# Hash attention followed by a mixture of adapters: two heads per unit in an order written by hand, 1024-column score tiles, attention output kept in SBUF, adapters run in batches inside the attention loop

## The chip, the cores and the metric

The kernel runs on one core of one Trainium2 chip. A core has a matrix engine (TensorE, PE in the profile, with its weight loads as PEld), a vector engine (VectorE, DVE), a scalar engine (ScalarE, ACT), a general engine (GpSimd, POOL), a synchronisation engine that here only starts DMA transfers (SyncE, SP), and 16 DMA engines. Each engine takes its instructions in order and waits on semaphores for what the others make. PE writes to PSUM, which has 8 banks of 2 KB per partition; the other engines empty PSUM into SBUF. The metric is device time in microseconds, and lower is better.

## What is computed

Four batches of eight heads, 768 positions, 64 features a head. Queries and keys are hashed by the signs of six projections; a query attends to the keys of its own bucket only. The 32 heads' outputs, laid side by side, are the input of a layer of eight low-rank adapters, of which each row takes the two with the highest gate.

```python
q_bits = (np.einsum('bhsd,dk->bhsk', q, proj) > 0)      # and k_bits
mask = q_bucket[:, :, :, None] == k_bucket[:, :, None, :]
scores = np.where(mask, scale * (q @ k.T), -1e9)
attn = exp(scores - max) / sum
x = (attn @ v) -> [B*S, H*D]                            # 3072 x 512
logits = x @ w_gate                                     # 8 experts, the 2 best
w = softmax of the two best logits
out = x + sum over the two: w * ((x @ A[e]) @ B[e])     # rank 16
```

## The kernel before

Everything is laid out by head, with a tile framework that decides the order of the instructions on each engine from the loops, the priorities and the pools' buffers. For each of the 32 heads the attention loop does the following. GpSimd starts three loads (vS, kS, qS; lines 81 to 85). PE transposes q and k, six blocks of 128 positions each, in float32 (lines 93 and 97); ACT copies the transposed k out of PSUM and DVE the transposed q. PE multiplies both with the projection in float32 (lines 104 and 107, 512 and 256 columns each, six output partitions), ACT takes the sign, and DVE scales it: the six scaled signs are rows 64 to 69 of kTaug and qTaug, under the 64 features in bfloat16 (lines 111 and 112). One product of 70 rows thus gives the score and a bonus that is largest where all six bits agree, and the bias neg_offset takes that bonus off again in the exponential.

The scores are made transposed, keys on the partitions: six tiles sc_ps of 128 keys by 768 queries (lines 117 and 118, 512 and 256 columns), each turned by one ACTIVATE on ACT into pTbuf (line 119). The pool of sc_ps has two buffers, so the next tile's product waits for the exponential two tiles back. Line 125 then multiplies, for each of six query blocks, six 128x128 pieces of pTbuf as weights with vS (80 columns, of which column 64 is a one and gives the row sum). DVE adds, inverts and scales (lines 130 to 134), and SP writes each 128x64 result to a DRAM tensor, x_bridge (line 135, 192 transfers).

Only behind the whole attention comes the adapter stage, in 24 tiles of 128 rows: SP reads 128x512 back (line 158), PE transposes it in four pieces (line 162) which ACT copies, then gate logits (line 167) and all eight low-rank products at once (line 174), a chain of small DVE operations for the two best gates with one exponential on ACT in it (lines 170 to 207), eight DVE scalings (line 211), a transpose (line 218), a copy on ACT, the product with B (line 222), the addition of x on DVE (line 224) and the store (line 226).

## Time and profile before

| | us |
|---|---|
| median of 3 runs | 540.51 |
| lowest and highest run | 538.18, 543.15 |
| the profiled execution's span, first to last instruction | 543.4 |
| until the first exponential starts | 18.5 |
| from there to the last sixth of the heads' loop (18.5 to 350) | 331.5 |
| the last head, alone (350 to 365) | 15.0 |
| the adapter stage (365 to the end) | 178.4 |

No time is shown for the profiled execution apart from its span; the span is 0.5% above the median of the runs. The page cuts the span into 40 slices and gives each engine's busy share of a slice in tenths, and PEclk, the TensorE clock that was granted, in tenths of its full 2.4 GHz. About the first 27 slices are attention: there PE is at 8 or 9 tenths, ACT at 5 to 8, DVE at 4 to 6, and PEclk at 6 to 9. The other 13 are the adapter stage, where PE is at 3 or 4, ACT at 1 or 2, DVE at 5 or 6, and PEclk at 5 throughout.

### The profile page before, as it was taken

The page shows a single profiled execution, that of the slowest core. Times are in us where ns is not written, and L with a number is a line of the kernel's source. Part 1 is how long each engine was busy: PE and PEld are TensorE (multiplying, and loading weights), DVE is VectorE, ACT ScalarE, POOL GpSimd, SP SyncE. Part 2 cuts the span into 40 slices and gives each one's busy share as a digit, 9 for nine tenths or more (in the row PEclk, how much of TensorE's full clock was granted, in tenths as well). Part 3 has the DMA queues.
Part 4 walks back from the last instruction along what each step waited for, and adds up shares of the span by engine and source line. Part 5 has one row for each costly group of instructions (what it writes and reads, how often), then busy time and mean ns, then how long its engine had stood idle before and what let it go on. Part 6 is the DMA issues. An engine that isn't in the chain of part 4 may idle for free.

```text
span 543.4 us, 8206 instructions
## 1 busy us (share of the span) xinstructions
PE 397.0 (73%) x2512; PEld 192.6 (35%) x2512; DVE 280.3 (52%) x1569; ACT 281.9 (52%) x529; POOL 86.3 (16%) x111
## 2 busy tenths in 40 slices
PE   4998889899999898899998998884333444433342
PEld 1444444443445444344444444342111222211121
DVE  2245546544445456345544564435656555565654
ACT  2656687857566877766657878652211222211121
POOL 9122222212112313211212221000000000000000
PEclk9999899969778999968869999855555555555555
DMA  8433343543232433423234333201222221122211
GB/s 100 50 66 60 70 69 68 114 76 67 51 60 56 76 71 77 71 54 57 54 56 76 70 71 39 27 18 54 70 79 77 77 78 66 56 74 77 77 59 40
DMA packets 68653, 35.43 MB, mean 65 GB/s; under 512 B 59264, under 2 KB 59392, under 8 KB 68608
## 3 DMA queue, kind: packets, MB, share of 16 engines
q0 software_dynamic: 34048, 16.01, 18.3%
q1 hardware_dynamic: 34560, 18.89, 12.3%
q8 instruction: 20, 0.33, 0.3%
q14 instruction: 25, 0.20, 0.1%
HBM read 25.71 MB, written 12.58 MB: 70 GB/s over the span
## 4 chain that ended last, share of the span: by engine, by line
PE 48%; ACT 28%; DVE 17%; issue 4%; DMA 1%; POOL 0%; ACTq 0%; DVEq 0%; POOLq 0%
ACT pTbuf L119 22%; PE pr L104 10%; PE ov_ps L125 9%; PE pr L107 8%; DVE zm L211 5%; PE sc_ps L117 4%; PE xT_ps L162 3%; PE d_ps L222 3%; ACT xT_sb L163 2%; PE zmT_ps L218 2%; PE z_ps L174 2%; PE tps L97 2%; PE tps L93 2%; ACT kTaug L105 2%; DVE qTaug L110 2%
## 5 line engine op out<-in xcount | busy, mean ns | idle before, releaser
L119 ACT ACTIVATE pTbuf<-sc_ps,neg_offset 128x768 bf16<-128x768 f32 x192 | 156.8, 906 | 55.1 <-PE sc_ps L118 54.7
L125 PEld LDWEIGHTS <-pTbuf 128*128 128x128 bf16 x1152 | 71.7, 107 | 130.8 <-DVE ores L134 47.9
L125 PE MATMUL ov_ps<-vS,pTbuf 128*128 128x80 bf16 x1152 | 99.6, 217 | 10.1 <-ACT pTbuf L119 7.5
L130 DVE TENSOR_SCALAR rsum<-ov_ps 128x1 f32<-128x1 f32 x192 | 26.7, 153 | 145.3 <-PE ov_ps L125 143.4
L117 PE MATMUL sc_ps<-qTaug,kTaug 70*128 70x512 bf16 x192 | 79.5, 415 | 20.5 <-ACT pTbuf L119 13.4
L218 PE MATMUL zmT_ps<-ident,zm 128*128 128x128 f32 x24 | 11.4, 474 | 89.7 <-DVE zm L211 89.7
L107 PE MATMUL pr<-qTf,proj_bf 64*6 64x256 f32 (+1 forms) x128 | 63.4, 581 | 0.0
L104 PE MATMUL pr<-kTf,proj_bf 64*6 64x256 f32 (+1 forms) x128 | 61.5, 566 | 0.0
L118 PE MATMUL sc_ps<-qTaug,kTaug 70*128 70x256 bf16 x192 | 56.3, 293 | 0.0
L134 DVE TENSOR_SCALAR ores<-ov_ps,rinv 128x64 f32<-128x64 f32 x192 | 50.6, 277 | 3.6 <-DMA x_bridge<-ores 2.6
L85 POOL DMA_DIRECT2D qS<-in_q_dram x32 | 26.6, 831 | 136.6 <-DVE rsum L130 86.4
L93 PE MATMUL tps<-ident,kS 128*64 128x128 f32 x192 | 42.0, 306 | 7.5 <-DMA kS<-in_k_dram 6.7
L105 ACT ACTIVATE kTaug<-pr 6x512 bf16<-6x512 f32 x64 | 30.6, 479 | 29.9 <-PE pr L104 28.7
L98 DVE COPY qTf<-tps 64x512 f32<-64x512 f32 x64 | 34.5, 538 | 16.2 <-PE tps L97 16.2
L219 ACT CAST zmT<-zmT_ps 128x128 bf16<-128x128 f32 x24 | 6.4, 266 | 70.2 <-PE zmT_ps L218 70.2
L108 ACT ACTIVATE qTaug<-pr 6x512 bf16<-6x512 f32 x64 | 30.6, 479 | 21.6 <-PE pr L107 20.2
L162 PE MATMUL xT_ps<-ident,xin 128*128 128x128 f32 x96 | 36.8, 435 | 3.4
L218 PEld LDWEIGHTS zmT_ps<-ident,zm 128*128 128x128 f32 x24 | 4.4, 183 | 96.0 <-DVE zm L211 96.0
L83 POOL DMA_DIRECT2D kS<-in_k_dram x32 | 26.5, 829 | 73.3 <-PE tps L93 68.6
L97 PE MATMUL tps<-ident,qS 128*64 128x128 f32 x192 | 37.7, 311 | 0.0
L163 ACT CAST xT_sb<-xT_ps 128x128 bf16<-128x128 f32 x96 | 24.3, 266 | 25.0 <-PE xT_ps L162 25.0
L224 DVE TENSOR_TENSOR acc<-d_ps,xin 128x512 f32<-128x512 f32 x24 | 16.6, 691 | 37.9 <-PE d_ps L222 37.9
(53 smaller groups left out, 443.2 us busy)
## 6 DMA issues: line engine op xcount, KB each, us to landing
kS<-in_k_dram POOLq DMA_DIRECT2D x32, 192.0 KB, 3.0
qS<-in_q_dram POOLq DMA_DIRECT2D x32, 192.0 KB, 3.1
x_bridge<-ores SPq DMA_DIRECT2D x192, 32.0 KB, 1.5
xin<-x_bridge SPq DMA_DIRECT2D x24, 256.0 KB, 2.7
out_dram<-acc SPq DMA_DIRECT2D x24, 256.0 KB, 2.0
vS<-in_v_dram POOLq DMA_DIRECT2D x32, 96.0 KB, 3.0
Acat<-in_moe_A_dram POOLq DMA_DIRECT2D x4, 32.0 KB, 3.0
Bcat<-in_moe_B_dram POOLq DMA_DIRECT2D x1, 128.0 KB, 3.2
```

The costliest lines, as they stand in the source:

```text
L93: nc.tensor.transpose(out=tps[:D, jj * P:(jj + 1) * P], in_=kS[:, j + jj, :], identity=ident)
L97: nc.tensor.transpose(out=tps[:D, jj * P:(jj + 1) * P], in_=qS[:, j + jj, :], identity=ident)
L104: nc.tensor.matmul(out=pr[:nbits, : hi - lo], lhsT=proj_bf, rhs=kTf[:, lo:hi], start=True, stop=True)
L105: nc.scalar.activation(out=kTaug[D:Daug, lo:hi], in_=pr[:nbits, : hi - lo], func=ACT.Sign, scale=1.0, bias=0.0)
L107: nc.tensor.matmul(out=pr[:nbits, : hi - lo], lhsT=proj_bf, rhs=qTf[:, lo:hi], start=True, stop=True)
L117: nc.tensor.matmul(out=sc_ps[:, :512], lhsT=kTaug[:, jk * P:(jk + 1) * P], rhs=qTaug[:, :512], start=True, stop=True)
L118: nc.tensor.matmul(out=sc_ps[:, 512:], lhsT=kTaug[:, jk * P:(jk + 1) * P], rhs=qTaug[:, 512:], start=True, stop=True)
L119: nc.scalar.activation(out=pTbuf[:, jk, :], in_=sc_ps, func=ACT.Exp, bias=neg_offset, scale=1.0)
L125: nc.tensor.matmul(out=ov_ps, lhsT=pTbuf[:, jk, iq * P:(iq + 1) * P], rhs=vS[:, jk, :], start=(jk == 0), stop=(jk == n_k_tiles - 1),)
L134: nc.vector.tensor_scalar_mul(out=ores, in0=ov_ps[:, :D], scalar1=rinv)
L162: nc.tensor.transpose(out=xT_ps, in_=xin[:, t * P:(t + 1) * P], identity=ident)
L163: nc.scalar.copy(out=xT_sb[:, t, :], in_=xT_ps)
```

## The change

The kernel is written anew as a class, Emitter, whose instructions keep the order in which they are written (the framework's scheduling is off; it still inserts the waits).

The unit is a pair of heads, 16 pairs p of 4 per batch. A pair's scores are 12 key tiles of 768 queries, taken as one row of 9216 columns and cut into nine slots of 1024 columns (two PSUM banks): score(p, s) makes two or three products and one ACTIVATE of 128x1024. PSUM: two buffers of two banks for the scores (tag s), two of one bank for transposes and hashes (tag t), one bank for the attention output (tag v) and one for all of the adapters (tag m). ACT does nothing but exponentials.

Between the slots' scores stands the other work, by slot s of pair p: s 0 and 1, transposes of pair p+1; s 2, 4, 5, the attention product of the second head of pair p-1 (14 products each); s 3, the hash of p+1; s 6, the first transposes of p+2 and a transpose of the finished output of p-2; s 7 and 8, the attention product of the first head of p (21 each). The casts, copies and normalisations on DVE go with them.

Parts of the computation change form. Two blocks of 64 features are transposed at once (128x128, 12 per pair instead of 24). The hash is four float32 products of 384 columns, each with 32 output partitions at its own strip of PSUM; DVE makes plus and minus one half of it in one operation, and eight small DMA transfers on SP's queue put the six sign rows under the features in `aug`. The feature scaling sits in the cast and in the exponential's scale, and a constant row replaces the bias. A seventh product per query block, with the constant eps as weights and the sum of v, is added. The output is normalised for six blocks at once into x, in SBUF; x_bridge is gone. v and x are cast on GpSimd. SP issues the loads, GpSimd only those of the adapter weights.

The adapters run on a batch of 768 rows, for batch b at pairs 4b+6 and 4b+7 (batches 0 to 2), and for batch 3 behind the loop: gate and low-rank products in one of 136 columns (lgz, three row blocks at a time), the gating for three blocks at once (route: DVE's max, two comparisons, an exponential on ACT, a product, three scalings), six transposes (zmtrans), and six times a product of 512 columns with one DVE operation (delta), each on the one bank of tag m.

```diff
+    def hash(self, p):
+        ps = self.ps_t.tile([self.P, 384], F32, tag="t", name=f"hs{p}")
+        for j in range(4):
+            nc.tensor.matmul(out=ps[32 * j:32 * j + 32, :], lhsT=self.proj2,
+                             rhs=self.qkT[p][:, j * 384:(j + 1) * 384], start=True, stop=True)
...
+        nc.vector.tensor_scalar(out=sgn, in0=ps, scalar1=0.0, scalar2=0.5,
+                                op0=ALU.is_gt, op1=ALU.subtract)
...
+        for j in range(4):
+            av = aug[64:70, j, :].rearrange("p (u e c) -> p u e c", e=2, c=self.P)
+            for e in range(2):
+                nc.sync.dma_start(out=av[:, :, e, :],
+                                  in_=sgn[32 * j + 6 * e:32 * j + 6 * e + 6, :].rearrange(
+                                      "p (u c) -> p u c", c=self.P))
...
+    def score(self, p, s):
...
+        ps = self.ps_s.tile([P, 1024], F32, tag="s", name=f"s{p}_{s}")
...
+            n = min(512 - at % 512, S - q0)
...
+        nc.scalar.activation(out=self.P_[p][:, s * 1024:end], in_=ps, func=ACT.Exp, scale=128.0)
...
+    def delta(self, b, i):
...
+        ps = self.ps_m.tile([P, self.Dm], F32, tag="m", name=f"dl{b}_{i}")
+        nc.tensor.matmul(out=ps, lhsT=self.zmT[b][:, i * P:(i + 1) * P], rhs=self.Bcat,
+                         start=True, stop=True)
+        nc.vector.scalar_tensor_tensor(out=self.acc[b][:, i, :], in0=ps, scalar=self.rt[b][:, i:i + 1],
+                                       in1=self.x[b][:, i, :], op0=ALU.mult, op1=ALU.add)
...
+    def moe_slot(self, p, s):
+        o = p - 2
+        if o >= 0 and o % self.PPB == 0 and o // self.PPB >= 1:
+            b = o // self.PPB - 1
+            if s in (1, 3):
+                self.lgz(b, s // 2)
+            if s in (2, 4):
+                self.route(b, s // 2 - 1)
+            if s == 5:
+                self.zmtrans(b)
+        o = p - 3
+        if o >= 0 and o % self.PPB == 0 and o // self.PPB >= 1:
+            b = o // self.PPB - 1
+            if s < 6:
+                self.delta(b, s)
...
+        for p in range(N):
+            for s in range(9):
+                self.score(p, s)
+                if s == 0:
+                    self.load(p + 2)
+                    self.norm(p - 1, 0)
+                    self.trans(p + 1, 1)
+                if s == 1:
+                    self.trans(p + 1, 2)
+                    self.vcast(p + 1)
+                if s == 2:
+                    self.pvmm(p - 1, 1, 0, 2)
+                    self.cast(p + 1, 0)
+                if s == 3:
+                    self.hash(p + 1)
+                if s == 4:
+                    self.pvmm(p - 1, 1, 2, 4)
+                    self.cast(p + 1, 1)
+                if s == 5:
+                    self.pvmm(p - 1, 1, 4, 6)
+                    self.norm(p - 1, 1)
+                if s == 6:
+                    self.trans(p + 2, 0)
+                    self.xtrans(p - 2)
+                if s == 7:
+                    self.pvmm(p, 0, 0, 3)
+                if s == 8:
+                    self.pvmm(p, 0, 3, 6)
+                self.moe_slot(p, s)
+        p = N - 1
+        self.norm(p, 0)
+        self.pvmm(p, 1, 0, 6)
+        self.norm(p, 1)
+        self.xtrans(p - 1)
+        self.xtrans(p)
+        b = self.B - 1
+        for g in range(2):
+            self.lgz(b, g)
+            self.route(b, g)
+        self.zmtrans(b)
+        for i in range(6):
+            self.delta(b, i)
```

On PE, before, the projection products of a head to come stand among the products of line 125, where the scheduler put them:

```order
L125 LDWEIGHTS pTbuf
L125 MATMUL ov_ps<-vS,pTbuf 128x80
L104 MATMUL pr<-kTf,proj_bf 6x256
L107 MATMUL pr<-qTf,proj_bf 6x256
L125 LDWEIGHTS pTbuf
L125 MATMUL ov_ps<-vS,pTbuf 128x80
```

After, in slots 3 and 4 of pair 1 (s is a score tile, hs the hash of pair 2, pv the output of pair 0):

```order
L190 LDWEIGHTS aug_106
L190 MATMUL s_3_382<-aug_106 128x512
L190 LDWEIGHTS aug_106
L190 MATMUL s_3_382<-aug_106 128x256
L190 LDWEIGHTS aug_106
L190 MATMUL s_3_382<-aug_106 128x256
L155 MATMUL hs_387<-qkT_263,proj_95 32x384 x4
L190 LDWEIGHTS aug_106
L190 MATMUL s_4_402<-aug_106 128x512
```

The four hash products now stand together, and the next slot's scores stand right behind them.

On DVE, before, one adapter tile's gating is a run of its own, nothing of the attention in it (20 instructions with the eight of line 211):

```order
L187 TENSOR_TENSOR l_6925<-l_6925,logits 128x8
L189 TENSOR_REDUCE m_6928<-l_6925 128x1
L191 TENSOR_SCALAR is_6930<-l_6925,m_6928 128x8
L197 TENSOR_SCALAR ssum<-w2p 128x1
L199 RECIPROCAL rinv<-ssum 128x1
```

After, in slots 2 to 4 of pair 6 (aug is the cast of pair 7, sgn its signs, lz and zm the adapters of batch 0):

```order
L172 TENSOR_SCALAR aug_106<-qkT_1208 64x12x128
L264 MAX top_0_1347<-lz_0_1311 128x8 x3
L266 TENSOR_TENSOR d_0_1351<-lz_0_1311,top_0_1347 128x24
L269 TENSOR_TENSOR m_0_1353<-lz_0_1311,top_0_1347 128x24
L274 TENSOR_TENSOR gw_0_1357<-m_0_1353,e_0_1355 128x24
L276 TENSOR_TENSOR zm_1345<-lz_0_1311,gw_0_1357 128x128 x3
L281 TENSOR_REDUCE ss_0_1362<-gw_0_1357 128x3
L282 RECIPROCAL rt_1346<-ss_0_1362 128x3
L158 TENSOR_SCALAR sgn_1375<-hs_1370 128x384
L172 TENSOR_SCALAR aug_106<-qkT_1208 64x12x128
```

A gating for 384 rows is now ten instructions between the two casts of the next pair, ahead of that pair's signs.

On SP, after, in slots 0 and 3 of each pair (the first three are the loads of pair p+2, the last the sign rows of pair p+1):

```order
L114 DMA nat_195<-in_q_dram 128x2x384
L114 DMA nat_195<-in_k_dram 128x2x384
L117 DMA vn_198<-in_v_dram 128x2x384
L164 DMA aug_106<-sgn_238 6x3x128 x8
L114 DMA nat_328<-in_q_dram 128x2x384
```

SP had one kind of transfer in the attention loop before, x_bridge; it now has these eleven per pair.

## Rows read from the trace of the kernel before

**Rows 1.** The page's first part: span, busy time, share of span and instructions.

```profile
span 543.4 us, 8206 instructions
PE 397.0 (73%) x2512; PEld 192.6 (35%) x2512; DVE 280.3 (52%) x1569; ACT 281.9 (52%) x529; POOL 86.3 (16%) x111
```

**Rows 2.** Windows by stage: length, busy PE, PEld, DVE, ACT, POOL (x instructions), PEclk, DMA.

```profile
18.50:350.00 331.50, 303.38 (x2067) 146.46 (x2065) 166.00 (x934) 233.57 (x367) 73.00 (x88) 0.90 0.35 65
365.00:543.40 178.40, 68.95 (x337) 35.46 (x336) 104.49 (x585) 35.56 (x140) 0.00 (x0) 0.50 0.20 67
```

**Rows 3.** Timeline of the adapter stage: start, length, instruction, [idle before].

```profile
480.48 0.61 PE L222 MATMUL d_ps<-Bcat,zmT 128*128 128x512 bf16 x1 [0.20 <-ACT zmT L219]
...
481.12 0.69 DVE L224 TENSOR_TENSOR acc<-d_ps,xin 128x512 f32<-128x512 f32 x1 [1.58 <-PE d_ps L222]
...
481.84 0.34 SPq L226 DMA_DIRECT2D out_dram<-acc  x1
...
486.92 0.48 PE L218 MATMUL zmT_ps<-ident,zm 128*128 128x128 f32 x1 [3.80 <-DVE zm L211]
```

**Rows 4.** Timeline, one head's run of exponentials: ACT, and PE within it.

```profile
205.31 4.86 ACT L119 ACTIVATE pTbuf<-sc_ps,neg_offset 128x768 bf16<-128x768 f32 x6 [1.44 <-PE sc_ps L118]
...
207.05 0.38 PE L117 MATMUL sc_ps<-qTaug,kTaug 70*128 70x512 bf16 x1 [0.23 <-ACT pTbuf L119]
...
207.27 0.27 PE L118 MATMUL sc_ps<-qTaug,kTaug 70*128 70x256 bf16 x1
...
207.38 0.24 PE L125 MATMUL ov_ps<-vS,pTbuf 128*128 128x80 bf16 x2
```

**Rows 5.** Groups of instructions by form, ACT: xcount, busy us, mean ns, idle before.

```profile
L119 ACT ACTIVATE pTbuf<-sc_ps,neg_offset 128x768 bf16<-128x768 f32 x192 | 156.8, 906 | 55.1 <-PE sc_ps L118 54.7
...
L108 ACT ACTIVATE qTaug<-pr 6x512 bf16<-6x512 f32 x32 | 18.7, 585 | 14.0 <-PE pr L107 14.0
...
L108 ACT ACTIVATE qTaug<-pr 6x256 bf16<-6x256 f32 x32 | 11.9, 372 | 7.6 <-PE pr L107 6.2
```

**Rows 6.** Timeline, PE between two runs of exponentials.

```profile
201.91 0.60 PE L125 MATMUL ov_ps<-vS,pTbuf 128*128 128x80 bf16 x12
...
202.44 0.59 PE L104 MATMUL pr<-kTf,proj_bf 64*6 64x256 f32 x2
...
202.87 0.59 PE L107 MATMUL pr<-qTf,proj_bf 64*6 64x256 f32 x2
...
205.55 0.60 PE L97 MATMUL tps<-ident,qS 128*64 128x128 f32 x4
```

**Rows 7.** Groups by form, DVE and one of POOL, columns as in rows 5.

```profile
L98 DVE COPY qTf<-tps 64x512 f32<-64x512 f32 x32 | 21.7, 679 | 13.6 <-PE tps L97 13.6
...
L112 DVE TENSOR_SCALAR qTaug<-qTf 64x768 bf16<-64x768 f32 x32 | 17.5, 547 | 0.0
...
L182 DVE TENSOR_REDUCE m<-logits 128x1 f32<-128x8 f32 x24 | 3.9, 161 | 0.8
...
masks.py:197 POOL MEMSET ident<- 128x128 f32 x1 | 0.2, 204 | 0.3 <-POOLq L241 0.3
```

**Rows 8.** DMA issues by line: xcount, KB each, median us from issue to landing.

```profile
kS<-in_k_dram POOLq DMA_DIRECT2D x32, 192.0 KB, 3.0
...
x_bridge<-ores SPq DMA_DIRECT2D x192, 32.0 KB, 1.5
```

**Rows 9.** Windows of 1 us around a fall of the granted clock, columns as in rows 2.

```profile
108.00:109.00 1.00, 0.98 (x8) 0.56 (x8) 0.00 (x0) 1.00 (x2) 0.00 (x0) 1.00 1.47 227
...
110.00:111.00 1.00, 1.00 (x2) 0.00 (x0) 0.00 (x0) 0.69 (x2) 0.00 (x0) 0.50 0.85 182
```

**Rows 10.** Timeline, the kernel's beginning.

```profile
6.70 1.03 PE L93 MATMUL tps<-ident,kS 128*64 128x128 f32 x4 [6.70 <-DMA kS<-in_k_dram]
...
11.53 0.94 DVE L112 TENSOR_SCALAR qTaug<-qTf 64x768 bf16<-64x768 f32 x1
...
13.85 1.06 PE L104 MATMUL pr<-kTf,proj_bf 64*6 64x256 f32 x2
```

425 lines of the change are left out of this document (252 added, 173 removed).

## Prediction

> **What bounds the kernel now.** I read the page's first part, then the windows by stage, then the timeline inside one stretch of each stage. The page alone misleads: PE is busy for 73% of 543.4 us and DVE and ACT for 52% each [rows 1], but these are means over two stages. The windows separate them [rows 2]. The attention loop (331.5 us from the first exponential, 18.5, to 350, then a last head of 15) has PE at 92%, ACT at 70%. The adapter stage takes 178.4 us, a third of the span, with no engine over 60% and the clock at 0.50, the lower level of 1.2 GHz.
>
> The adapter stage is a latency chain: 24 tiles of 128 rows in 178.4 us are 7.4 each, and in each PE waits 3.80 for DVE's small operations before it can transpose their result in L218 [rows 2, 3].
>
> The attention loop alternates. In a run of six exponentials (4.86 us) ACT sets the pace, and PE is held back: the products L117 wait for an exponential [rows 4]. Between the runs ACT waits for the projections and signs of the next head. A head is (331.5+15)/32 = 10.8 us on average, of which exponentials are 4.9; its 192 ACTIVATEs are 156.8 busy of ACT's 281.9 [rows 1, 5]. The rest of ACT's work is copies and signs, which the change takes away.
>
> **Prices.** ACT: a lone 128x768 exponential takes 0.91 and six 4.86, so one follows another in (4.86-0.91)/5 = 0.79 [rows 4, 5]. From 256 to 512 columns ACT goes from 0.372 to 0.585, 0.83 ns a column [rows 5]; 256 columns more make 0.79+0.21 = 1.00 per 1024-column slot, 1.12 alone. PE at the upper level: the 512-column product starts 0.22 ahead of the 256-column one, this 0.11 ahead of the next, and lasts 0.16 longer than that (its drain) [rows 4]; so a slot's scores are 0.44, ready for ACT 0.2 later. Twelve products of line 125 take 0.60, so 0.037 each without the drain; scaled from 80 to 65 columns 0.030; I take 0.034. Four transposes: 0.60-0.16, 0.11 each (weights are now 128 columns instead of 64; serial loads would double it, and I keep 0.11 as in the row). A 256-column float32 product starts 0.43 ahead of the next, in two records (x2) [rows 6]; 384 columns: 0.64.
>
> **The hash.** Four such products write four strips of PSUM. No row shows products into different strips. Bounds: 0.64, all four beside each other; 2.6, one after another as lines 104 and 107 run. The two records of one product share a strip, so I let only a product's first pass overlap the second of the one ahead: five of eight passes, 1.6. I take 1.6, in the middle. By the Trainium skill (TensorE: Matmul & The Clock Gate, Part 3: Packing small matmuls) matmuls in different column strips run concurrently, their starts about 4 ns apart. No run here shows it; by that the hash would be 0.65 and the sum 214, the second rival below.
>
> **One pair.** PE: scores 9x0.44 = 4.0, 84 products 2.9, twelve transposes 1.3, hash 1.6, six bfloat16 transposes 0.3 (0.42 ns a column from the row of line 125): 10.1. ACT: 9.0. DVE takes 0.16 for its smallest operation and 0.68 for a 512-column copy out of PSUM, so 1.0 ns a column, and half of that in the cast of line 112 (0.547 for 768 columns), so 0.95 for one of 1536 [rows 7]: three copies 2.0, signs 0.55, two casts 1.9, two normalisations 1.4, one 768-column copy 0.94: 6.8. POOL: 2,176 columns a pair at 204 ns for 128 [rows 7]: 3.5. So PE and ACT set the pace, DVE and POOL hide beneath them.
>
> Order decides what is lost between those two. A slot's scores may start when the exponential two slots back has ended, 1.15 after its start, and are ready 0.44+0.2 later, at 1.79; ACT wants them at 2.00. PE can thus be 0.21 late. By slot, PE needs its scores' 0.44 and, in slots 0 and 1, four transposes (0.88 each); in 2, 4 and 5, 14 products (0.92); in 3 the hash (2.05); in 6, four transposes and six small ones (1.2); in 7 and 8, 21 products (1.15). Slot 3, with the hash, is 1.05 over ACT's 1.00 and costs 0.84; slots 6 to 8 are 0.5 over and cost 0.35; the short slots only restore the spare 0.21. A pair is 9.0+0.84+0.35 = 10.2, for two heads that took 21.7. Sixteen: 163.
>
> SP now issues three loads and eight sign transfers a pair, 3.7 us at 0.34 [rows 3], and POOL no longer issues any in the loop; the 216 transfers through x_bridge fall away, and with them nothing on the path but the first wait of the adapter stage. The signs must make the pair's time too. Signs are done 0.75 after slot 3 (4.7), eight issues are 2.7, landing 1.5 as x_bridge [rows 8]: 9.7 of 10.2. It is covered by half a microsecond; at the 3.0 that the loads take [rows 8] it costs 1.0 a pair, 15 in all.
>
> **Adapters in the loop, three batches.** In pair 4b+6 the second lgz (12 products of 136 columns, 0.7) needs the one bank of tag m back. Followed from slot 2: DVE's cast 0.95, three max at 0.16, two comparisons 0.34, the exponential there and back 0.45, a product 0.17, three scalings 0.8 end at 3.2 to 3.5; PE stands behind its hash at 2.95 and waits; slot 4 starts 1.2 late. The same chain, with sgn and cast ahead of it on DVE, ends at 7.4; the transposes of zm wait for it in slot 5 and those of x in slot 6 for the copy (0.94): 4.0 lost. In pair 4b+7 DVE has its 6.8 and six deltas at 0.69 [rows 3], 10.9 in all, and each delta's product waits for the bank of the one before, so that PE follows DVE through slots 0 to 5: 2.85 lost. Together 6.85, three times 20.5. This is where the removed stall of 3.80 a tile goes: from 24 times to 6, with PE's scores queued behind it, and ACT behind those.
>
> **Head and tail.** First transposes at 6.7 as now, twelve at 1.03/4 [rows 10] end at 9.7, copy 0.7, hash at the lower level (two records 1.06 less drain for 256 columns) 3.2, sign 0.65, transfers 4.1: first score at 18.3. The first slots run at the lower level, +2. Behind the last exponential: normalise 0.7, product 1.6, normalise 0.7, POOL's cast 1.2, transposes and copy 1.6, lgz 1.6, route 2.6, lgz 1.6, route 2.6, transposes and copy 1.7, six deltas at 1.33 (L222 at 480.48 to the end of L224 at 481.81 [rows 3]; one bank, so serial) 8.0, store 2.3: 26.
>
> **Sum.** 18.3+2+163+20.5+26, less 1 as the last pair has no hash: 229, against the span of 543.4. The runs' median lies 0.5% below that span; so 228.
>
> **Rivals.**
> - Forecast, 215 to 243: 0.50.
> - Strips overlap: slot 3 needs 1.1 and costs nothing, a pair is 9.3: 214. For it: separate strips in one bank; against: two passes per product. 0.17, with its own spread 200 to 215.
> - The hash is serial (11.2 a pair, 244), or its transfers land at 3.0 (243), or POOL slows DVE: L112 took 0.94 at 11.53, while POOL issued loads, against 0.55 [rows 7, 10], and doubled casts (+1.6 a pair) would be hidden in a plain pair but add about 10 in the six adapter pairs. 243 to 258: 0.20.
> - The clock falls. It did so behind a run of exponentials with PE partly waiting: 1.00 at 108, 0.50 at 110 [rows 9], and the loop's mean is 0.90, a fifth of the time low [rows 2]. A pair at the lower level is 20, PE's 10.1 doubled; with a fifth of the loop there, T/5/20+4T/5/10.2 = 16 pairs gives T = 181 for 163: 246. With low clock throughout: 16x20+80, 400. Against: outside adapter pairs PE here waits 0.1 of 10.2. 0.11. The Trainium skill (same page, A second HAM failure mode) speaks against this change: PE that idles briefly while cycling through PSUM buffers goes back and forth between the two levels. The falls in rows 9 agree with it.
> - Slower than before: the eight sign transfers land strictly one behind another. At t each, a pair is 5.5+8t, and 16 pairs with 46 of head and tail exceed 540 from t = 3.2 on. Loads land in 3.0, so it is not far; but a 192 KB load alone makes 64 GB/s, and the engines moved 227 in one window [rows 8, 9], so transfers overlap. 0.01. That the adapter stage stays as it is can't be: it now works on 768 rows at a time.
>
> Below 200, 0.05; above 262, 0.10: low clock with serial hash, and something not seen, to which the last 0.01 also goes. **Faster** by over 1% (what a measurement of this kernel can tell from no change) holds in all but the last: 0.97; same 0.01, slower 0.02. Range 200 to 262.
>
> **What the profile would show.** Right: exponentials of 1.1 us, 16 pairs of 10, the longest PE stretch in slot 3; four L155 products (eight records) in 1.6; ACT's idle time released by L190 products; pairs 6, 10, 14 about 14 us and the next about 13; a tail of 26 with PEclk 0.50. Wrong: a pair of 9.3 with L155 in 0.7; PEclk of 0.9 or less in the loop; scores waiting for DMA (signs late); PE in plain pairs waiting for DVE, or casts of 1.7.

## The result

The kernel after takes 219.87 us (median of 4 runs, 218.24 to 221.41), the kernel before in the same measurement 539.35 (535.63 to 543.15): a ratio of 0.407, with a 95% interval of 0.404 to 0.411. 228.0 was predicted, with a range of 200 to 262. The profiled execution is the one of 218.24; its span is 216.4, so 1.8 us lie around it. The executions of some of the kernels below fall into two groups a few per cent apart; where they do, the single times are given.

The page's first part, to be held against [rows 1], with the slices of the granted clock:

```profile
span 216.4 us, 5569 instructions
...
PE 178.0 (82%) x2288; PEld 123.5 (57%) x2288; DVE 142.9 (66%) x303; ACT 144.1 (67%) x153; POOL 63.4 (29%) x98
...
PEclk9995569999999999999999999999999999997555
```

The span is 0.40 of the span before and PE's busy time 0.45 of it: the change removed work (the 24 small transposes of a pair became 12, and the adapters' 24 tiles became 4 batches) as well as waiting. PE is now busy in 82% of the span. The granted clock is at its lower level, 1.2 GHz, or between the two in slices 4 to 6 (16 to 32 us) and in the last four, and at 2.4 GHz or close to it in slices 7 to 36. The nines of the first three slices say little: this trace has no record of the clock before 13.3 us, and the view counts such a stretch as full speed. Four transposes take 1.12 us at 8.74, about as long as the 1.06 at 18.59, where the recorded clock is the lower one.

The windows by stage (columns as in [rows 2]):

```profile
0.00:18.80 18.80, 7.83 (x28) 3.78 (x29) 12.28 (x18) 1.28 (x1) 12.16 (x26) 0.94 0.85 142
18.80:29.00 10.20, 9.94 (x38) 4.99 (x38) 4.66 (x6) 6.95 (x7) 3.41 (x4) 0.50 0.35 118
...
40.00:78.70 38.70, 38.34 (x555) 27.92 (x552) 26.70 (x46) 35.51 (x38) 15.26 (x23) 1.00 0.39 128
78.70:101.00 22.30, 19.52 (x252) 13.62 (x250) 18.84 (x49) 16.16 (x18) 4.68 (x8) 1.00 0.41 134
...
191.70:216.40 24.70, 9.13 (x90) 5.13 (x90) 10.77 (x34) 0.50 (x3) 0.83 (x1) 0.62 0.16 64
```

The first row is the head, until the first exponential (18.5 us before, now 18.8). In the second, PE is busy throughout and at 0.50. The third is four plain pairs (2 to 5): PE 38.34 of 38.70 us, 99%; ACT, which the prediction had at the same pace, 92%. The fourth is an adapter pair and most of the next, with PE at 88%, DVE at 84% and ACT at 72%. The last row is what is left of the adapter stage of 178.4 us: 24.7.

The costliest groups of the page:

```profile
L193 ACT ACTIVATE P<-s 128x1024 bf16<-128x1024 f32 x144 | 141.6, 1024 | 47.1 <-PE s L190 43.6
L190 PE MATMUL s<-aug 71*128 71x512 bf16 (+1 forms) x384 | 89.9, 336 | 5.0 <-DMA aug<-sgn 4.8
...
L155 PE MATMUL hs<-qkT,proj 128*32 128x384 f32 x128 | 15.8, 542 | 0.0
```

ACT is idle for 47.1 us, and 43.6 of it end with a score's product: ACT waits for PE. The hash's 64 products (128 records, two for each) show no idle time ahead of them.

One plain pair in the timeline (start, length, instruction, [idle before]); 50.83 is the first exponential of pair 3, 69.31 that of pair 5, 78.69 that of pair 6, 91.70 that of pair 7:

```profile
50.83 3.77 ACT L193 ACTIVATE P<-s 128x1024 bf16<-128x1024 f32 x4 [0.68 <-PE s L190]
...
51.01 0.60 PE L190 MATMUL s<-aug 71*128 71x512 bf16 x2
...
51.44 0.60 PE L144 MATMUL tr<-ident,nat 128*128 128x128 f32 x4
...
51.90 0.59 PE L190 MATMUL s<-aug 71*128 71x256 bf16 x3
...
52.33 0.35 PE L209 MATMUL pv<-vb,P 128*128 128x65 bf16 x6
...
52.82 0.59 PE L190 MATMUL s<-aug 71*128 71x512 bf16 x3
...
53.34 0.85 PE L155 MATMUL hs<-qkT,proj 128*32 128x384 f32 x8
...
54.13 0.61 PE L190 MATMUL s<-aug 71*128 71x512 bf16 x2
...
54.85 6.20 SPq L164 DMA_DIRECT2D aug<-sgn  x8
...
56.78 0.50 PE L238 MATMUL xtp<-ident_bf,xb 128*128 128x128 bf16 x6
...
57.12 0.60 PE L190 MATMUL s<-aug 71*128 71x512 bf16 x2
```
```profile
78.69 1.94 ACT L193 ACTIVATE P<-s 128x1024 bf16<-128x1024 f32 x2 [0.33 <-PE s L190]
...
91.70 1.02 ACT L193 ACTIVATE P<-s 128x1024 bf16<-128x1024 f32 x1
```

Read from start to start, PE's prices stand there: a slot's scores 0.43 (51.01 to 51.44), four transposes 0.46 (to 51.90), fourteen products of line 209 0.49 (52.33 to 52.82), the four hash products 0.79 (53.34 to 54.13), the six small transposes 0.34 (56.78 to 57.12). A pair's nine slots, twelve transposes, 84 products, hash and small transposes are 9x0.43+3x0.46+6x0.49+0.79+0.34 = 9.3. By the starts of the exponentials in the trace, a plain pair that no transfer delays takes 9.20 to 9.27, so little but PE's own time is in it; pairs 3 and 4 together take the 18.48 from 50.83 to 69.31. Pairs 6, 10 and 14 take 13.01 (78.69 to 91.70 is the first of these), pairs 7 and 11 12.34, pair 0 13.23.

### The profile page after: what moved, and what is told of

Its sections match the earlier page's. It is cut to its first block, busy times and chain, and to the rows that moved or that the text cites. A ratio compares the mean times of both kernels' runs of the same rounds, so it can differ in the third digit from the quotient of the medians.

```text
span 216.4 us, 5569 instructions
## 1 busy us (share of the span) xinstructions
PE 178.0 (82%) x2288; PEld 123.5 (57%) x2288; DVE 142.9 (66%) x303; ACT 144.1 (67%) x153; POOL 63.4 (29%) x98
## 4 chain that ended last, share of the span: by engine, by line
PE 52%; DVE 22%; DMA 9%; SPq 8%; issue 5%; ACT 2%; POOLq 0%; POOL 0%; DVEq 0%
PE s L190 20%; PE pv L209 12%; SPq L164 7%; PE tr L144 7%; PE hs L155 5%; DVE acc L303 5%; DMA nat<-in_k_dram 5%; PE dl L301 3%; DMA aug<-sgn 3%; DVE aug L172 3%; DVE sgn L158 2%; PE xtp L238 2%; DVE zm L276 2%; DMA nat<-in_q_dram 2%; DVE x L225 2%
## 5 line engine op out<-in xcount | busy, mean ns | idle before, releaser
L193 ACT ACTIVATE P<-s 128x1024 bf16<-128x1024 f32 x144 | 141.6, 1024 | 47.1 <-PE s L190 43.6
L190 PE MATMUL s<-aug 71*128 71x512 bf16 (+1 forms) x384 | 89.9, 336 | 5.0 <-DMA aug<-sgn 4.8
L209 PEld LDWEIGHTS <-P 128*128 128x128 bf16 x1152 | 51.3, 98 | 14.8 <-DVE x L225 1.0
L209 PE MATMUL pv<-vb,P 128*128 128x65 bf16 x1152 | 53.8, 194 | 0.9 <-DVE x L225 0.9
L190 PEld LDWEIGHTS <-aug 71*128 71x128 bf16 x384 | 32.5, 100 | 28.8 <-issue 13.0
L229 POOL CAST xb<-x 128x768 bf16<-128x768 f32 x16 | 13.2, 825 | 115.3 <-DVE x L225 115.3
L147 DVE COPY qkT<-tr 128x512 f32<-128x512 f32 x48 | 33.0, 690 | 14.1 <-PE tr L144 12.5
L144 PE MATMUL tr<-ident,nat 128*128 128x128 f32 x192 | 32.9, 296 | 8.1 <-DMA nat<-in_q_dram 3.9
L209 PE MATMUL pv<-vb,eps 128*128 128x65 bf16 x192 | 37.4, 195 | 0.0
L144 PEld LDWEIGHTS tr<-ident,nat 128*128 128x128 f32 x192 | 25.2, 152 | 14.4 <-issue 5.6
L172 DVE TENSOR_SCALAR aug<-qkT 64x1536 bf16<-64x1536 f32 x32 | 31.9, 998 | 0.9
L209 PEld LDWEIGHTS <-eps 128*128 128x128 bf16 x192 | 18.9, 98 | 0.0
L126 POOL CAST vb<-vn 128x768 bf16<-128x768 f32 x16 | 13.3, 833 | 13.7 <-DMA vn<-in_v_dram 13.7
L155 PE MATMUL hs<-qkT,proj 128*32 128x384 f32 x128 | 15.8, 542 | 0.0
```

Of the source, the lines that this page charges most:

```text
L144: nc.tensor.transpose(out=ps[:, j * P:(j + 1) * P], in_=self.nat[p][:, idx % 2, idx // 2, u * P:(u + 1) * P], identity=self.ident)
L147: nc.vector.tensor_copy(out=self.qkT[p][:, g * 512:(g + 1) * 512], in_=ps)
L155: nc.tensor.matmul(out=ps[32 * j:32 * j + 32, :], lhsT=self.proj2, rhs=self.qkT[p][:, j * 384:(j + 1) * 384], start=True, stop=True)
L172: self.nc.vector.tensor_scalar(out=av[:, :, e, :], in0=self.qkT[p][64 * e:64 * e + 64, :].rearrange("p (j c) -> p j c", c=self.P), scalar1 ...
L190: nc.tensor.matmul(out=ps[:, o:o + n], lhsT=aug[0:71, 2 * h + 1, kt * P:(kt + 1) * P], rhs=aug[0:71, 2 * h, q0:q0 + n], start=True, stop=True)
L193: nc.scalar.activation(out=self.P_[p][:, s * 1024:end], in_=ps, func=ACT.Exp, scale=128.0)
```

## The experiments

**The hash in full width.** Do four products into four strips of PSUM run beside each other? Each product gets 128 output columns of weights instead of 32, so that all four must use the whole array. The number of products and their columns stay.

```diff
+        self.proj4 = sg.tile([P, P], F32, name="proj4")
+        for j in range(4):
+            nc.vector.tensor_copy(out=self.proj4[:, 32 * j:32 * j + 32], in_=self.proj2)
...
-            nc.tensor.matmul(out=ps[32 * j:32 * j + 32, :], lhsT=self.proj2,
+            nc.tensor.matmul(out=ps, lhsT=self.proj4,
```

> Each of the four hash products is given 128 output columns (the projection four times side by side) instead of 32, so all four write the same 128 partitions and none can run beside another; the number of records, columns and everything behind is as in the changed kernel. The last product's signs stand for all, so the masks are not the reference's. Theory 1 (the four strips run beside each other, which is why the hash takes 0.78 us and not 1.6): the hash goes to four times 0.64, 2.6 us, slot 3 of a pair from 1.2 to 3.0, a plain pair from 9.2 to 11.0, 15 hashes in the loop and a slow one at the start: 244 to 250 us. Rival (float32 products of this size run in 0.2 us each whatever strips they write): hash 0.8, time 218 to 222.

Measured: 240.98 us (one run), 21 more, under the 244 to 250 expected. The same place in a plain pair:

```profile
59.91 2.75 PE L158 MATMUL hs<-qkT,proj 128*128 128x384 f32 x8
62.49 0.60 PE L193 MATMUL s<-aug 71*128 71x512 bf16 x2
```

The eight records now take 2.58 us to the next scores, against 0.79 in strips. 2.58 is the serial price that the prediction had as its upper bound (2.6), and 0.79 is near the lower (0.64). A plain pair takes 10.90 instead of 9.21, 1.69 more for the 1.8 more of the hash, so hardly any of it was hidden there. The three adapter pairs 6, 10 and 14 lose only 0.8 each and pair 8 nothing, and so the whole grew less than expected. The single records show the overlap itself. In full width the eight start one after another, 0.32 us apart; in strips four of them start within 0.02 us, 6 to 7 ns apart, and the other four together 0.35 us later. The strips do run beside each other; with a serial hash the kernel would stand at 241.

**Without the seventh product.** Is a plain pair bound by PE or by ACT? The product with eps is left out, and with it the value of rows without a key in their bucket; 12 of 84 products per pair.

```diff
-            for kt in range(T + 1):
+            for kt in range(T):
...
-                                 start=(kt == 0), stop=(kt == T))
+                                 start=(kt == 0), stop=(kt == T - 1))
```

> The seventh product of each query block (constant weights, sum of v) is left out, 192 of 1344 products, with it the term that stands for rows without a matching key. Theory 1 (a plain pair's 9.2 us is the sum of PE's work, PE never waits in it): 12 products of 0.032 us less a pair, 0.39, over 16 pairs 6.1, 213 to 215 us. Rival (the exponentials pace the loop, PE's work fits beneath): within 1 us of the changed kernel, 219 to 221.

Measured: 214.74 us (213.87 to 215.96), ratio to before 0.397 (0.393 to 0.400). A plain pair takes 8.95. That is 0.26 less, where twelve products at 0.035 are 0.42. Slots 6 to 8, which take longer than an exponential, become shorter by 0.07 to 0.10 each: there PE sets the pace. Slots 2, 4 and 5 were at 0.90 to 0.92 and are at 0.90 to 0.92 still, though PE has only 0.43 and twelve products, 0.85, in each: there the exponential does.

```profile
40.00:78.70 38.70, 38.49 (x520) 27.76 (x518) 27.26 (x47) 36.86 (x39) 16.22 (x24) 1.00 0.40 128
```

In this window ACT rises from 35.51 to 36.86 busy, in the same length as above. Both engines are near their limit, and the pitch of a run of 1024-column exponentials is read here: 0.90, where the prediction had 1.00.

**768 columns.** What is the 1024-column tile worth by itself? The scores go back to 12 tiles of 768 columns per pair, two products each; the rest of the order stays.

```diff
-        at, end = s * 1024, (s + 1) * 1024
...
+        h, kt = divmod(s, self.T)
+        for q0, n in ((0, 512), (512, 256)):
...
-            for s in range(9):
-                self.score(p, s)
+            for s12 in range(12):
+                self.score(p, s12)
+                s = {0: 0, 1: 1, 3: 2, 4: 3, 5: 4, 7: 5, 8: 6, 10: 7, 11: 8}.get(s12)
```

> Score tiles of 768 columns, twelve slots a pair instead of nine, the same products (24 a pair), the other work spread over the twelve in the same order. Theory 1 (PE sets a plain pair with 9.2 us; exponentials of 768 columns follow one another in 0.79, twelve are 9.5): a pair goes to 9.5, at most 9.8, about 5 us more in all: 222 to 229. Rival (larger tiles are what removed ACT's overhead, and with 192 instead of 144 exponentials the loop grows by their whole cost of 0.15 each and by waits in each): 230 or more. Second rival (ACT has slack in either form): 218 to 221.

Measured: 224.98 us (223.96 to 225.48), 5 more than the kernel after. A plain pair takes 9.79, 0.58 more; an adapter pair 0.1 to 0.2 more. Three exponentials of a plain pair in the timeline, and the group of all:

```profile
59.28 2.21 ACT L188 ACTIVATE P<-s 128x768 bf16<-128x768 f32 x3 [0.27 <-PE s L186]
```
```profile
L188 ACT ACTIVATE P<-s 128x768 bf16<-128x768 f32 x192 | 144.3, 810 | 48.9 <-PE s L186 48.5
```

One takes 0.81, and three in a row 2.21, so one follows another in 0.70. The same size took 0.91 and 0.79 in the kernel before [rows 4, 5]. From 0.81 to the 1.02 of 1024 columns the slope is 0.84 ns a column, and from 0.70 to 0.90 0.78. A pair's twelve exponentials at 0.70 are 8.4, nine of 1024 at 0.90 are 8.1: the wider tile takes 0.3 off ACT's time in a pair. How much of the 0.58 that is, and how much comes from the order of the other work in twelve slots, this run does not separate. Of the 320 us that the change brings, the tile's width accounts for 5.

**All four batches of adapters behind the loop.** What is the place of the adapters inside the loop worth?

```diff
-                self.moe_slot(p, s)
...
-        b = self.B - 1
-        for g in range(2):
...
+        for b in range(self.B):
+            for g in range(2):
+                self.lgz(b, g)
+                self.route(b, g)
+            self.zmtrans(b)
+            for i in range(6):
+                self.delta(b, i)
```

> All four adapter batches run behind the attention loop, one after the other, in the same form; x and its transpose have four buffers, acc one. Theory 1 (in the loop a batch costs 3.8 and 3.1 us of PE's and ACT's time, behind it some 16 us at the lower clock, as the last batch shows from 196.7 to 212.8): the loop loses 18 us, the tail gains three times 16: 246 to 252 us. Rival (batching alone brings the gain, the place does not matter): 218 to 225.

Measured: 248.42 us (one run), within the 246 to 252 expected.

```profile
41.00:171.40 130.40, 127.46 (x1847) 92.85 (x1845) 85.86 (x148) 120.89 (x126) 44.22 (x64) 1.00 0.35 115
171.40:246.60 75.20, 31.35 (x198) 16.23 (x198) 36.21 (x121) 1.78 (x8) 0.83 (x1) 0.54 0.21 84
```

The loop ends 20.4 us earlier (171.36 for 191.76), the tail is 75.2 instead of 24.7, at a clock of 0.54. So three batches cost 20 in the loop and 50 behind it. Inside the loop they are not hidden; they are 2.5 times cheaper there, where the loop's work fills a part of the chain's waits and the clock stays at 1.00.

**Two banks for the adapters.** Does the adapter pairs' loss come from the one bank of tag m? Tag t gives one of its two banks to tag m.

```diff
-        self.ps_t = ps("ps_t", 2)
+        self.ps_t = ps("ps_t", 1)
...
-        self.ps_m = ps("ps_m", 1)
+        self.ps_m = ps("ps_m", 2)
```

> One bank goes from tag t (transposes and hashes, two to one) to tag m (adapters, one to two). Theory 1 (the 3.8 and 3.1 us that an adapter pair loses come from the single bank of tag m): pairs 6, 10, 14 go from 13.0 to about 11 and pairs 7 and 11 from 12.3 to about 10.5, the last deltas from 1.43 to about 0.8 each, in all 10 to 13 us less; against it each transpose waits for the copy of the one before, at most 0.3 in slots 0 and 1, 16 times: 208 to 214 us. Rival (DVE's order and load set those pairs, the bank only shows it): the adapter pairs stay at 12 to 13, plain pairs grow to 9.6 or more: 219 to 228.

Measured: 216.75 us (216.38 to 216.88), 3 less than the kernel after, between the two expectations. The total mixes in something else: pair 8 takes 14.55 instead of 11.01 and pair 12 10.85 instead of 9.39, both in slot 6 (4.19 and 2.28), where a load is late; pair 8's fall of the clock is in the last section. The parts separate the cases better. The tail is 18.9 instead of 24.7, and pair 7 10.89 instead of 12.34: there the bank was the wait. Pair 6 takes 13.10, as before, 3.4 over its own plain pair: its slot 3, with the second lgz, is 0.66 shorter, but slots 1 and 4 are 0.56 and 0.67 longer, so what the bank alone is worth there this run does not separate. Plain pairs pay for it with 9.73, since the transposes of slot 1 now wait for the copy of slot 0's. What PE waits for in pair 6 is in the kernel after's timeline:

```profile
81.87 0.85 PE L155 MATMUL hs<-qkT,proj 128*32 128x384 f32 x8
...
82.58 0.69 DVE L276 TENSOR_TENSOR zm<-lz,gw 128x128 bf16<-128x128 f32 x3
...
83.32 0.89 PE L250 MATMUL lz<-wa,xT 128*128 128x136 bf16 x12 [0.59 <-DVE zm L276]
...
84.04 0.60 PE L190 MATMUL s<-aug 71*128 71x512 bf16 x2
...
87.02 0.51 PE L290 MATMUL ztp<-ident_bf,zm 128*128 128x128 bf16 x6 [1.05 <-DVE zm L276]
...
87.37 0.60 PE L190 MATMUL s<-aug 71*128 71x512 bf16 x3
```

Behind the hash, PE waits 0.59 for the first gating's last scaling (L276) before the second lgz, and 1.05 for the second gating before the transposes of zm. The scores of slots 4 and 6 (84.04, 87.37) stand behind these on PE's queue, and ACT behind the scores. A second bank changes nothing in the second of the two, which waits for the result itself.

**The tail's banks.** Only for the last batch, and only with banks that are free by then: its deltas go into the score buffers, its second lgz into tag t, and both lgz stand ahead of the gating.

```diff
+        pool, tag = (self.ps_t, "t") if b == self.B - 1 and g == 1 else (self.ps_m, "m")
+        lz = pool.tile([P, 3, self.LZ], F32, tag=tag, name=f"lz{b}_{g}")
...
+        pool, tag = (self.ps_s, "s") if b == self.B - 1 else (self.ps_m, "m")
+        ps = pool.tile([P, self.Dm], F32, tag=tag, name=f"dl{b}_{i}")
...
         for g in range(2):
             self.lgz(b, g)
+        for g in range(2):
             self.route(b, g)
```

> Behind the loop the last batch's six deltas take the two score buffers, which are free by then, and its second gate product takes a bank of tag t, ahead of the first gating. Theory 1 (the last batch's deltas are 1.43 us apart, product 0.6 and DVE 0.75 in turn, because they share one bank; the second gate product waits 1.8 for DVE): deltas come at DVE's pace, 0.8, 3.2 less; the second gating starts 1.5 earlier: 215 to 217. Rival (DVE's latency chain sets the tail): 1 us or less, 218 to 220.

Measured: 213.26 us, the median of 210.80, 211.76, 214.76 and 215.56; the profiled one is that of 211.76. In the kernel after the deltas stood one behind the other in PE and DVE:

```profile
199.39 1.54 PE L250 MATMUL lz<-wa,xT 128*128 128x136 bf16 x12 [1.82 <-DVE zm L276]
...
204.23 0.61 PE L301 MATMUL dl<-Bcat,zmT 128*128 128x512 bf16 x1 [0.65 <-DVE zmT L293]
205.68 0.58 PE L301 MATMUL dl<-Bcat,zmT 128*128 128x512 bf16 x1 [0.84 <-DVE acc L303]
```
```profile
204.88 0.75 DVE L303 SCALAR_TENSOR_TENSOR acc<-dl,rt,x 128x512 f32<-128x512 f32 x1 [0.70 <-PE dl L301]
```

That is 1.43 a delta. With more banks DVE runs them without a gap:

```profile
202.02 4.26 DVE L305 SCALAR_TENSOR_TENSOR acc<-dl,rt,x 128x512 f32<-128x512 f32 x6 [0.70 <-PE dl L303]
```

Six take 4.26, and the tail 19.3 instead of 24.7. That is 5.4 of the 6.5 by which the two profiled executions differ. Most of the rest is the clock: in this profile pair 0 took 9.95 instead of 13.23, and against that pair 14 took 14.56 instead of 13.01. Both are taken up below.

**Loads one pair earlier.** Pair 8 took 11.01 in the kernel after, though it is a plain one. In the chain of waits (start, us, what):

```profile
104.20 0.78 SPq L114
...
105.03 6.56 DMA nat<-in_k_dram
...
111.63 0.33 PE tr L144
```

The load of k for pair 10 was issued in slot 0 of pair 8, behind the stores of batch 0 on SP's queue, and landed 6.56 later, after the transposes of slot 6 wanted it.

```diff
-        self.natp = ctx.enter_context(tc.tile_pool(name="natp", bufs=3))
+        self.natp = ctx.enter_context(tc.tile_pool(name="natp", bufs=4))
...
+        self.load(2)
...
-                    self.load(p + 2)
+                    self.load(p + 3)
```

> Each pair's loads are issued one pair earlier, with four buffers instead of three. Theory 1 (slot 6 of pair 8 takes 2.96 instead of 1.16 because pair 10's k, issued behind eight sign transfers of 0.72 us each on SP, lands too late; pair 2's last slot, 1.70, likewise): 2 us less, 217 to 219, if the third load at the start does not delay the first signs; SP issues three loads more there, 1.4 us, which fall before the signs are ready. Rival (the stall comes from contention among the transfers, not from when they are issued): it stays: 219 to 221.

Measured: 217.08 us (215.74 to 217.96), 2.8 less. Pair 8 takes 9.21, as a plain pair should, and pairs 5 and 12 do too (9.39 before). Pair 2 takes 10.49 now (9.88 before): the first scores of pair 3 wait 1.11 for the sign transfers, where it was 0.35. Pair 0 takes 14.29, with the low clock until 32.6 instead of 30.4 us. The stall is gone, and a smaller one at the start came in its place; the two profiled executions differ by 0.4 only, so the 2.8 of the medians is not shown part by part.

**Dummy products at the start.** Pair 0 takes 13.23 us, 4.0 more than a plain pair, at the lower clock. Is this because PE pauses before it? Sixteen and twelve products of 512 columns, which nobody reads, go before the first transposes and behind the first hash.

```diff
+    def warm(self, n):
+        for i in range(n):
+            w = self.ps_s.tile([P, 1024], F32, tag="s", name=f"w{self.nw}")
...
+            for c in range(2):
+                nc.tensor.matmul(out=w[:, 512 * c:512 * c + 512], lhsT=self.eps, rhs=self.wrm,
+                                 start=True, stop=True)
```

> PE runs products on constants into the score banks while it waits at the start: 16 of 512 columns ahead of the first transposes and 12 between the first hash and the first scores; nothing else changes. Theory 1 (pair 0 takes 13.2 instead of 9.2 us, and the first hash 2.3 instead of 0.8, because the granted clock is at the lower level until 29 us): the clock is at the upper level by the first scores, pair 0 falls to 9 to 10, the hash to 0.8 or at worst stays: 4 to 6 us less, 214 to 216. Rival (pair 0 is long because its loads and sign transfers are late): no change, 219 to 221.

Measured: 215.51 us, the median of two pairs of runs: 212.12 and 212.49, 218.52 and 218.97. The profiled one is that of 218.97. In it the clock was at 1.00 from 6.7 to 16.9 us, and the first hash took 1.69 instead of 2.35. But then PE waited 1.89, until 16.72, for the sign transfers of pair 0, the clock was at 0.50 from 16.9 to 30.6, and pair 0 took 13.62. So these products raised the clock and did not hold it; whether holding it is worth the 4 us is left to the last two experiments.

**The adapters spread over four pairs.** If PE's standing behind DVE's chain is the loss, the same work in other slots should lose less. lgz and route of batch b go into pairs 4b+5 and 4b+6, so that a product on the bank of tag m comes two slots or more behind DVE's step, the deltas into pairs 4b+7 and 4b+8 (all six into pair 15 for batch 2), and the transposes of x move to slot 8 of the next pair.

```diff
+            f = self.PPB * b + self.PPB + 1
...
+            if p == f and s == 1:
+                self.lgz(b, 0)
+            if p == f and s == 2:
+                self.route(b, 0)
+            if p == f and s == 8:
+                self.lgz(b, 1)
+            if p == f + 1 and s == 0:
+                self.route(b, 1)
+            if p == f + 1 and s == 5:
+                self.zmtrans(b)
```

> The adapters of batches 0 to 2 are dealt out over four pairs instead of two, so that no product on the bank of tag m follows a VectorE step of the same batch by less than two slots: both products lgz in pair 4b+5 (slots 1 and 8), the gatings right behind them (slot 2 and the next pair's slot 0), the transposes of zm in pair 4b+6, the deltas three each in pairs 4b+7 and 4b+8 (all six in pair 15 for batch 2). The transposes of x come earlier, in slot 8 of the next pair. The work is the same. Theory (an adapter pair loses its 3.8 and 3.1 us because TensorE, in order, stands behind VectorE's chain): what is left per batch is TensorE's own time, 24 products of 136 columns at 0.06, six transposes at 0.055 and six deltas at 0.22, 3.0 us for 6.9, three times: 208 us (206 to 211). Rival (VectorE's own time, 9 us a batch, cannot be hidden, or its wait for the small exponential behind a slot's large one stalls the casts): no gain, 217 to 221.

Measured: 216.58 us (215.68 to 216.75), 3.3 less than the kernel after, of the 12 expected, and just under the rival's 217 to 221. By pairs, 5 to 8 take 42.5 instead of 45.8, in which the 1.8 of pair 8's late load is gone, 9 to 12 take 44.4 instead of 44.0, and 13 to 15 32.8 as before. As it stood, the spread bore out the rival more than the theory. With the tail's banks and the early loads added:

> The spread adapters, with the two edits measured one by one before: the last batch's deltas in the score buffers and both its lgz ahead of the gating (tail 24.7 to 19.3 us) and the loads one pair earlier (the late load of pair 8, 1.8 us). If the three add, 208 less 5 less 2: 201 us (198 to 204). Rival: the parts don't add, since the earlier loads slow the start (pair 0 took 14.3 us with them against 13.2), and 203 to 207 comes out. If the spread gains nothing: 210 to 213.

Measured: 209.59 us (209.29 to 210.70). The two edits brought 7.0 on top of the spread, as much as their 5.4 and 1.8 of the traces, but the spread itself fell short, so the sum did: 201 was expected, with 198 to 204, and the result lies above the rival's 203 to 207 too. Against the kernel with early loads alone, pairs 5 to 15 take 118.3 instead of 120.3. Its profile shows where:

```profile
78.89 0.50 PE L238 MATMUL xtp<-ident_bf,xb 128*128 128x128 bf16 x6
80.03 0.87 PE L251 MATMUL lz<-wa,xT 128*128 128x136 bf16 x12 [0.65 <-DVE xT L240]
...
84.70 1.21 PE L155 MATMUL hs<-qkT,proj 128*32 128x384 f32 x8
85.84 0.60 PE L190 MATMUL s<-aug 71*128 71x512 bf16 x2
```

The second lgz now waits 0.65 for DVE's copy of the transposed x that shares its bank; the gating in slot 0 of the next pair stands on DVE ahead of the last of the three copies of the transposed q and k (84.35), and so the hash takes 1.21 instead of 0.85. Pairs 5 to 8 lose 2.84, 1.14, 0.87 and 1.02 (12.04, 10.34, 10.07 and 10.22 less 9.20): 5.9 for a batch, where 6.9 was lost in two pairs before and PE's own added time is 3.1 (24 products of lgz at 0.06, six transposes 0.34, six deltas at 0.22).

Next, PE is kept busy up to the first scores: the dummy products, sixteen ahead of the first transposes and sixteen right ahead of the first scores, in this same kernel.

> The kernel with spread adapters, tail and loads, and TensorE kept busy until the first scores by 16 and 16 products of 512 columns that nobody reads, the second 16 right ahead of the first score. Theory (the low clock of the first 10 us of attention comes from TensorE's pauses before it): the clock is 1.00 from 18 to 29 us in every execution, the first pair takes 9 to 10 us instead of 13, and all times lie within 1% some 4 us under the kernel without the dummy products: 195 to 199. Rival (what decides it is not TensorE's activity here): the executions fall into two groups 4 to 6 us apart, as they did with fewer dummy products, or none gains.

Measured: 205.75 us (203.27 to 208.40), 3.8 less. In the profiled run pair 0 took 10.07 instead of 14.26, with the lower clock from 18.2 to 21.6 us only, behind waits of PE of 1.11 and 0.66 for the sign transfers. But the times neither lie within 1% nor in the 195 to 199 expected: the six runs lay at 203.3, 203.5, 205.3, 206.2, 208.3 and 208.4, with mean granted clocks of 0.981, 0.973, 0.964, 0.957, 0.943 and 0.934 in the same order; the five of the kernel without dummy products lay at 0.920 to 0.940. The dummy products raise the clock, most of the time and not always. Whether it is PE's pauses or something that only goes with them is not settled.

Last, the two waits just named are removed: the second lgz, its gating and the transposes of zm move on to slots 1, 2 and 6 of pair 4b+6.

```diff
-            if p == f and s == 8:
+            if p == f + 1 and s == 1:
                 self.lgz(b, 1)
-            if p == f + 1 and s == 0:
+            if p == f + 1 and s == 2:
                 self.route(b, 1)
-            if p == f + 1 and s == 5:
+            if p == f + 1 and s == 6:
                 self.zmtrans(b)
```

> The kernel with spread adapters, tail, loads and dummy products, with the second lgz, its gating and the transposes of zm moved on (to slots 1, 2 and 6 of pair 4b+6). In the kernel with the spread adapters the four pairs of a batch lost 2.84, 1.14, 0.87 and 1.02 us against a plain pair of 9.20, 5.9 together where TensorE's own added work is 3.1; the largest single waits were the second lgz behind VectorE's copy of the transposed x (slot 8 of pair 4b+5) and the hash and scores behind the gating's place among the copies (slots 0 to 3 of the next). Theory (these two waits make the 2.8 us of excess): pairs 4b+5 and 4b+6 take 10.1 and 10.5 instead of 12.05 and 10.34, a batch loses 4.1 to 4.4, the whole gains 4.5 to 5.5 us: 200 to 202. Rival (the excess is VectorE's load and comes back wherever the gating stands): 204 to 207, as without the move.

Measured: 199.68 us (198.48 to 204.89), ratio to before 0.371 (0.369 to 0.374), and 0.91 of the kernel after: this is the best kernel of the study. The six runs lay at 198.5, 199.3, 199.4, 200.0, 201.5 and 204.9. That is 6.1 less than before the move by the medians and 5.1 by the four fastest of each. The two profiled executions differ by 5.4: pairs 5 to 15 give 3.9, under the 4.5 to 5.5 expected of the move; the start gives 2.1, since pair 0 took 8.78 and had no low clock at all; the tail takes 0.6 back. Pairs 5 to 8 take 10.74, 9.96, 10.01 and 10.06 (10.1 and 10.5 were expected for the first two), so the first batch loses 4.0, the second 5.0 (pair 9 takes 11.47). With this the theory of the spread is right in kind: PE's own 3.1 is most of what a batch still loses.

```profile
28.00:63.30 35.30, 35.30 (x527) 26.12 (x526) 23.83 (x42) 32.68 (x35) 13.40 (x19) 1.00 0.43 140
63.30:104.10 40.80, 40.47 (x575) 29.16 (x574) 32.32 (x75) 35.67 (x39) 13.67 (x21) 1.00 0.45 147
104.10:145.00 40.90, 39.52 (x565) 28.34 (x564) 31.87 (x73) 35.21 (x38) 13.04 (x20) 1.00 0.47 159
```
```profile
114.84 0.61 PE L193 MATMUL s<-aug 71*128 71x512 bf16 x3 [0.93 <-DMA aug<-sgn]
```

The plain pairs (pair 1 from 28 us on, and 2 to 4) have PE busy in 35.30 of 35.30 us, the adapter pairs 5 to 8 in 40.47 of 40.80, and 9 to 12 in 39.52 of 40.90, where the first scores of pair 10 wait 0.93 for their sign transfers. What is left in the loop is nearly all PE's own work.

## Why the prediction came out as it did

The time fell in the range and among the 215 to 243 of the forecast, 8 us under the value. That it did owes something to luck: the plain pairs are 15.6 us less than costed, and 7.7 of terms that were costed too low or at nothing (the start, the late transfers, the time around the span) went the other way. The terms, against the profiled execution:

| term | predicted | measured |
|---|---|---|
| head (first score predicted, first exponential measured) | 18.3 | 18.8 |
| low clock at the start | +2 | +4.0 (pair 0: 13.23 less 9.21) |
| 16 plain pairs | 163 (10.2 each) | 147.4 (9.21 each) |
| three batches of adapters | +20.5 | +19.8 (3.80 and 3.13 twice, 3.80 and 2.1 in pairs 14 and 15) |
| late transfers (pairs 2, 5, 8 and 12) | 0 | +2.9 |
| last pair, and pair 1 without small transposes | -1 | -1.1 |
| tail | 26 | 24.7 |
| span | 229 | 216.4 |
| around the span | -1 | +1.8 |

**Right.** The two stages, the removal of the 178 us chain, the size of the adapter pairs (4.0 and 2.85 predicted, 3.80 and 3.13 measured), the tail (26 and 24.7) and the prices of PE's work came out: scores 0.44 (0.43), four transposes 0.44 (0.46), a product of line 209 0.034 (0.035). The tail's largest term was L222 to L224 at 1.33 [rows 3] six times over, because of the one bank; it is 1.43. That the bank is the wait is shown for the tail and for pair 7 by the kernel with two banks; for the second lgz of pair 6 it is not separated, and the larger wait there, 1.05 ahead of the transposes of zm, is for the gating itself, as predicted. Two prices of the prediction were off without an effect: the row of line 125, 0.037 for 80 columns, gives 0.46 ns a column and not 0.42 (the six bfloat16 transposes take 0.34, for 0.3), and DVE's 768-column copy takes 0.55 and not 0.94.

**The plain pair was mis-sized, by two terms.** The hash was taken at 1.6, in the middle of its bounds; it takes 0.79. No row of before showed strips, and the split of the difference (a product's first pass beside the second of the one ahead) was an invention: in the trace four of the eight records run at once, then the other four. So of the rivals, the one with a chance of 0.17 had the mechanism: the strips overlap and a pair takes 9.3 (9.21). Such a pair, with L155 in 0.7, is also the first sign that the prediction gave of being wrong. That rival's 214 is under the 218.2 of the profiled run mostly by the start (2 more than costed), the late transfers (2.9) and the time around the span (2.8), from which the smaller tail and plain pair take back 2.7. By the Trainium skill (TensorE: Matmul & The Clock Gate, Part 3: Packing small matmuls) the hash would have been 0.65; the trace, with 0.79 against 2.58 in full width, agrees with the rule; the other 0.14 is not explained.

The second term is the exponential's pitch, taken at 1.00: 0.79 [rows 4] and 256 columns more at 0.83 ns [rows 5]. The slope was right (0.84 in the kernel with 768 columns); the base was not, for the same 128x768 takes 0.70 there. What differs in the rows is the operand neg_offset, the bias, which stands in the row of before and is gone in the rows of after; that it is the bias that costs the 0.1 was not tried apart. With 0.90 a pair's exponentials are 8.1, under PE's sum of 9.2, and the alternation that I had argued (ACT sets 9.0, PE may be 0.21 late) hardly matters: a plain pair is PE's sum.

**The sign transfers were nearer to the path than costed.** They take 0.72 us each on SP's queue (eight in 6.20, at 54.85) and not the 0.34 of a store [rows 3]. By the prediction's own sum (signs done at 5.5, which is 0.75 behind slot 3's 4.7, then eight issues, then 1.5 to land) that would be 5.5+6.2+1.5 = 13.2, more than a pair. That this costs next to nothing was not foreseen: the first head's scores need only the first four transfers, and those of the second head stand four slots later. On PE's side the scores wait for them 4.8 us in all, 4.4 of it in the first two slots of pair 0 and 0.35 at the end of pair 2, which is among those that are late.

**The start and the loads.** The low clock was costed at 2, for the first slots; it held until 30.4 us, for nearly all of pair 0, which takes 4.0 more. The loads were costed at nothing; that they stand in SP's queue behind the adapters' stores, and must land within six slots, was not looked at. Pair 8 alone loses 1.8 by it.

**The clock.** The rival of a falling clock (0.11) did not come true in the kernel after. From 40 us to the last exponential the granted clock is 1.00, in plain and in adapter pairs, where PE is busy in 88%; before, it was 0.90 with PE at 92% [rows 2]. The Trainium skill (TensorE: Matmul & The Clock Gate, A second HAM failure mode: psum-queue depth-cycling) speaks of a clock that goes back and forth where PE pauses briefly while it cycles through PSUM buffers. The kernel does cycle so, and in this trace the pauses of 0.6 to 1.05 us of the adapter pairs brought no fall. In two other traces they were followed by one. The kernel with the tail's banks has the same pair 14, and there PE waits 0.60, 1.05 and 0.48 and is busy for 1.23 of 2.60 us before the clock falls:

```profile
173.00:175.60 2.60, 1.23 (x15) 0.93 (x16) 2.16 (x9) 1.54 (x2) 0.74 (x1) 1.00 0.03 8
175.60:178.60 3.00, 3.00 (x32) 2.04 (x30) 0.56 (x1) 1.31 (x2) 0.08 (x1) 0.50 0.03 6
```

That pair took 14.56 instead of 13.01, and with the dummy products at the start it took 14.55 in the same way. So the risk that the rival named is there, in an adapter pair; it cost 1.5 us where it came, and why it came in pair 14 and not in pairs 6 and 10 is not shown.

**The rival of the other sign** needed 3.2 us for each sign transfer, one behind another. They are issued 0.72 apart, and all eight in 6.2 of a pair's 9.2.

## What to carry to other kernels

Four small products into different strips of one bank cost 0.79 here, near the 0.64 worked out for one and far from the 2.58 of all four in full width; price them so and try it with one run in full width. In a kernel whose order is written by hand, a product that waits for a short chain of another engine costs its wait for everything queued behind it: deal such a chain out over the units, with each product two slots behind what it needs and on a bank that nothing else has just filled (here, with the loads early, pairs 5 to 15 went from 120.3 to 114.0 us by it; the rest of the way from 219.9 to 199.7 is the tail's banks, the earlier loads and the clock at the start). A price taken by interpolation between two bounds is a guess; where a term decides between two rivals, the chances should say so.
